# Reordering the first tiles of an attention and GLU kernel: split first load, square root first, copies on one engine, K by chunk

## The chip, the cores and the metric

The kernel runs on one core of a Trainium2 chip. The metric is the device time in microseconds (us) of an execution. Each execution also has a **span**, from its first to its last instruction, given to 0.1 us. Engines: PE (TensorE; PEld is its weight load, which overlaps), VectorE (DVE), ScalarE (ACT), GpSimd (POOL), SyncE (SP).

## The reference, cut to what matters

```python
xn = layernorm(x)                      # x: 1 x 2048 x 640, bf16
qkv = xn @ wqkv                        # wqkv: 640 x 1920
# 32 heads of 20; each position attends to 8 positions, 2 apart
o = softmax(q . k over the window) applied to v
out = x + o @ wo + ((xn @ w_gate) * (xn @ w_up)) @ w_down    # hidden width 1536
```

## The kernel before

The 2048 rows are 16 tiles of 128. Each tile gets a layernorm in place; tiles 0 to 3 are then transposed on PE through PSUM and copied to SBUF, the later ones by transposing transfers. Q and K of the first tiles are projected tile by tile while the rest of x is still normalised. The contraction of 640 goes in five chunks of 128, and the weights of Q and of K come in five loads each, one per chunk.

```python
x_load(1, "act"); x_load(0)                 # tile 1 on ScalarE's queue, tile 0 on SyncE's
for c in range(5): wqkv_load(0, c)          # Q's weight chunks, SyncE
x_load(2); x_load(3)
for c in range(5): wqkv_load(1, c)          # K's weight chunks, SyncE
...
def ln_aggr(t):                             # tiles other than 1: statistics on VectorE
    bn_aggr(mv, st)                         # DVE
    activation(sd, mv[:, 1:2], Sqrt)        # ACT
def ln_sums(t, k):                          # tile 1: sum (k=0), squares (1), square root (2) on ACT
    ...
def ln_copy(t, ...):                        # PSUM -> SBUF after the transposes
    parts = ((("act", 0, 1), ("dve", 1, 3), ("act", 3, 5)),    # tile 0
             (("dve", 0, 2), ("act", 2, 5)),                   # tile 1
             (("act", 0, 5),), (("act", 0, 5),))[t]
...
warm(10)                                    # 10 matmuls of 512 columns on zeros
ln_stats_a(0); ln_stats_b(0)
ln_sums(1, 0)
ln_aggr(0)
ln_sums(1, 1); ln_sums(1, 2)
ln_apply(0); ln_pe(0); ln_copy(0)           # normalise, transpose, copy
ln_apply(1)
warm(2, 128)
# then Q of tile 0 (tile 1 transposed after its chunk 2), Q of tile 1, K of tile 0
# (tile 2 transposed after chunk 2), K of tile 1 (tile 3 transposed after chunk 3)
```

Each instruction waits only for what its operands need.

## Time and profile before

| | before |
|---|---|
| time, median of the first 3 executions | 254.13 us (254.0 to 254.83) |
| span of the profiled one | 252.5 us |
| PE busy, share of the span | 249.1 us, 99% |
| first projection of tile 0 starts | 6.18 us |
| first projection of tile 2 starts | 12.68 us |
| PE's last work ends | 250.19 us |

PE works without a break from the first transpose on. So the end of PE is the start of its useful work plus a fixed 244 us, unless a gap opens. Two markers tell how the opening went: the first projection of tile 0, and the first projection of tile 2, by which the whole rearranged part is over. The order of SyncE's transfers (start, length of issue, what, count):

```profile
0.75 0.40 SPq L293 DMA_DIRECT2D XST<-in_A_x_dram  x1
1.20 2.33 SPq L293 DMA_DIRECT2D WQKV<-in_A_wqkv_dram  x5
3.57 0.91 SPq L293 DMA_DIRECT2D XST<-in_A_x_dram  x2
4.52 2.33 SPq L293 DMA_DIRECT2D WQKV<-in_A_wqkv_dram  x5
```

Q's five weight chunks are issued from 1.20 us on, one each 0.47 us; K's from 4.52.

### The profile page before, as it was taken

To read this page: it belongs to the slowest core of one execution; us is meant where nothing else is said; L and a number is where in the kernel's file an instruction comes from. 1 tells how busy PE (TensorE), PEld (TensorE's weight loads), DVE (VectorE), ACT (ScalarE), POOL (GpSimd) and SP (SyncE) were. 2 spreads that over 40 slices of the span, in tenths; PEclk is the share of its full clock that TensorE was granted. 3 is DMA by queue.
4 is the path that set the end of the run, shared out by engine and by line. 5 is a ranking of instruction groups with operands and counts; after the bars stand their busy time and mean duration, and the time that the engine had idled before them with its cause. 6 is when DMAs were issued, how large, how long until landed. Compare 5 with 4: busy or idle time off the path is not lost.

```text
span 252.5 us, 3929 instructions
## 1 busy us (share of the span) xinstructions
PE 249.1 (99%) x1623; PEld 149.3 (59%) x1623; DVE 214.7 (85%) x251; ACT 114.8 (45%) x204; POOL 35.9 (14%) x44
## 2 busy tenths in 40 slices
PE   8999999999999999999999999999999999999996
PEld 3999855555544444444444457764445777777775
DVE  4799999999999854999999974999999999993221
ACT  6577775555555557555555553135555112112000
POOL 1000001044515430003411110100000010111000
DMA  6969889956677471536379940393000021330511
GB/s 195 330 144 175 120 217 373 280 116 120 122 145 125 83 139 29 201 132 124 57 137 319 435 108 6 37 348 55 0 0 0 3 28 24 55 44 10 104 52 53
DMA packets 25649, 31.84 MB, mean 126 GB/s; under 512 B 9856, under 2 KB 22144, under 8 KB 25600
## 3 DMA queue, kind: packets, MB, share of 16 engines
q1 hardware_dynamic: 19104, 22.07, 28.4%
q0 software_dynamic: 6240, 9.31, 23.1%
q8 instruction: 12, 0.20, 0.3%
q10 hardware_dynamic: 288, 0.23, 0.3%
q14 instruction: 5, 0.04, 0.0%
HBM read 14.42 MB, written 4.59 MB: 75 GB/s over the span
## 4 chain that ended last, share of the span: by engine, by line
PE 99%; DVE 0%; issue 0%
PE PS L643 41%; PE PS L674 29%; PE PS L471 17%; PE PS L486 4%; PE PS L497 2%; PE PS L504 2%; PE PS L449 2%; PE PS L430 1%; DVE FOUT L688 0%; DVE ZERO L296 0%; DVE EPSC L297 0%
## 5 line engine op out<-in xcount | busy, mean ns | idle before, releaser
L643 PE MATMUL PS<-XNT,WG 128*128 128x512 bf16 x240 | 59.6, 379 | 0.0
L643 PE MATMUL PS<-XNT,WU 128*128 128x512 bf16 x240 | 59.6, 379 | 0.0
L610 DVE TENSOR_TENSOR PVB<-VO,ATB 128x10240 f16<-128x10240 bf16 x8 | 43.9, 5486 | 0.1
L471 PE MATMUL PS<-XNT,WQKV 128*128 128x512 bf16 x200 | 43.3, 379 | 0.0
L674 PE MATMUL PS<-WD,HT 128*128 128x320 bf16 (+2 forms) x300 | 43.2, 294 | 0.0
L643 PEld LDWEIGHTS PS<-XNT,WU 128*128 128x128 bf16 x240 | 23.5, 98 | 28.3
L643 PEld LDWEIGHTS PS<-XNT,WG 128*128 128x128 bf16 x240 | 23.5, 98 | 28.1
L645 ACT ACTIVATE USX<-PS 128x512 bf16<-128x512 f32 x48 | 28.7, 597 | 22.2 <-PE PS L643 21.2
L674 PEld LDWEIGHTS PS<-WD,HT 128*128 128x128 bf16 x300 | 28.7, 98 | 11.0
L471 PEld LDWEIGHTS PS<-XNT,WQKV 128*128 128x128 bf16 x200 | 23.5, 118 | 19.5
L605 DVE TENSOR_TENSOR PVB<-PVB 128x5120 f16<-128x5120 f16 (+1 forms) x16 | 34.5, 2154 | 0.3
L538 POOL DMA_DIRECT2D LOG<-PE x24 | 21.7, 931 | 59.6 <-DMA LOG<-PE 59.6
L645 ACT ACTIVATE HT<-PS 128x512 bf16<-128x512 f32 x36 | 21.5, 597 | 16.7 <-PE PS L643 16.7
L683 ACT ACTIVATE FACC<-PS 128x640 f16<-128x640 f32 x12 | 8.5, 704 | 45.4 <-PE PS L674 45.4
L674 PE MATMUL PS<-WO,VO 128*128 128x320 bf16 (+2 forms) x165 | 27.1, 295 | 0.0
L674 PEld LDWEIGHTS PS<-WO,VO 128*128 128x128 bf16 x165 | 15.9, 98 | 6.0
L527 DVE TENSOR_TENSOR PP<-QH,KH 128x2048 f16<-128x2048 bf16 x16 | 19.1, 1216 | 0.0
L527 DVE TENSOR_TENSOR TMP<-QH,KH 128x2048 f16<-128x2048 bf16 x16 | 19.0, 1216 | 0.0
L532 DVE TENSOR_TENSOR PP<-PP,TMP 128x4096 f16<-128x4096 f16 x8 | 18.3, 2288 | 0.2
L688 DVE TENSOR_TENSOR FOUT<-PS,XR 128x320 bf16<-128x320 f32 (+2 forms) x9 | 4.1, 454 | 16.6 <-PE PS L674 16.6
L698 POOL DMA_DIRECT2D out_dram<-FACC x6 | 7.1, 1186 | 76.5 <-ACT FACC L683 76.5
L538 POOL DMA_DIRECT2D PE<-PP x8 | 8.7, 1090 | 60.7 <-DVE PP L533 60.7
(67 smaller groups left out, 229.5 us busy)
## 6 DMA issues: line engine op xcount, KB each, us to landing
PE<-PP POOLq DMA_DIRECT2D x8, 512.0 KB, 5.0
ATB<-LOG SPq DMA_DIRECT2D x8, 512.0 KB, 4.8
LOG<-PE POOLq DMA_DIRECT2D x24, 128.0 KB, 2.7
WG<-in_B_w_gate_dram SPq DMA_DIRECT2D x5, 384.0 KB, 6.2
WU<-in_B_w_up_dram SPq DMA_DIRECT2D x5, 384.0 KB, 12.4
WD<-in_B_w_down_dram SPq DMA_DIRECT2D x1, 1920.0 KB, 10.0
out_dram<-in_A_x_dram SPq DMA_DIRECT2D x1, 1920.0 KB, 9.4
out_dram<-FACC POOLq DMA_DIRECT2D x6, 320.0 KB, 4.7
```

What stands on the lines that cost most here:

```text
L471: op("pe", (lambda l, x, c: lambda e: e.matmul(PS[:, b, :], l, x, start=(c == 0), stop=(c == NCH - 1)))(l, x, c), r=[l, x], w=[PS[:, b, :] ...
L486: op("pe", (lambda o, l, x, st, sp: lambda e: e.matmul(o, l, x, start=st, stop=sp))(o, l, x, st, sp), r=[l, x], w=[o], name=f"pp{which}_{m ...
L527: return (1.22, lambda: op("dve", lambda e: e.tensor_tensor(o, qw, kw, ALU.mult), r=[q, k], w=[o], name=f"prod{h}_{p}_{c}"))
L532: (2.3, lambda: op("dve", lambda e: e.tensor_tensor(a, a, b, ALU.add), r=[a, b], w=[a], name=f"psum{h}_{p}")),
L538: op("pool", lambda e: e.dma_start(o, i, accum_op=ALU.add), r=[o, i], w=[o], dma=True, name=name)
L605: return lambda: op("dve", lambda e: e.tensor_tensor(o, x, y, ALU.add), r=[x, y], w=[o], name=f"{name}_{b}")
L610: lambda: op("dve", lambda e: e.tensor_tensor(PVB[:], vw, aw, ALU.mult), r=[v, a], w=[PVB[:]], name=f"pv_{b}")),
L643: op("pe", (lambda l, x, c: lambda e: e.matmul(PS[:, b, :], l, x, start=(c == 0), stop=(c == NCH - 1)))(l, x, c), r=[l, x], w=[PS[:, b, :] ...
L645: op("act", lambda e: e.activation(o, PS[:, b, :], ACT.Copy), r=[PS[:, b, :]], w=[o], name=f"guev{which}_{m}_{j}")
L674: op("pe", (lambda l, x, i, b, wid: lambda e: e.matmul(PS[:, b, 0:wid], l, x, start=(i == 0), stop=(i == n - 1)))(l, x, i, b, wid), r=[l, ...
L683: op("act", (lambda o, i: lambda e: e.activation(o, i, ACT.Copy))(o, i), r=[PS[:, b - 1, :], PS[:, b, :]], w=[o], name=f"fin{t}")
L698: stores.append(op("pool", lambda e: e.dma_start(d, f, accum_op=ALU.add), r=[f, ("out",)], w=[("out", t)], dma=True, name=f"oacc{t}"))
```

## The change

The intent is to start the useful work of PE earlier. Tile 0 comes in two halves on two queues; its square root goes ahead of tile 1's sums on ScalarE; its copies all go to VectorE, so that none waits behind those sums; tile 1 is transposed later, in two pieces; K of tiles 0 and 1 is done chunk by chunk for both tiles together. The diff, cut to its core:

```diff
-    x_load(1, "act")
-    x_load(0)
+    for half, eng in ((0, "sp"), (1, "act")):
+        dst = XST[:, 0, half * DHALF:(half + 1) * DHALF]
+        dma(dst, xhbm[0:TS, half * DHALF:(half + 1) * DHALF], w=[dst], name=f"xh{half}", eng=eng)
+    x_load(1)
     for c in range(NCH):
         wqkv_load(0, c)
...  (w_gate and w_up: one transfer each instead of five; each half's statistics read their half only)
-        for c0, c1 in ((0, 128), (128, D)) if t == 0 else ((0, D),):
+        for c0, c1 in {0: ((0, 128), (128, D)), 1: ((0, 256), (256, D))}.get(t, ((0, D),)):
...
-        parts = ((("act", 0, 1), ("dve", 1, 3), ("act", 3, NCH)), ...
+        parts = ((("dve", 0, 1), ("dve", 1, 3), ("dve", 3, NCH)), ...
...
-    warm(10)
+    warm(9)
     ln_stats_a(0)
     ln_stats_b(0)
+    ln_aggr(0)
     ln_sums(1, 0)
-    ln_aggr(0)
...  (Q and K of tiles 0 and 1)
+    proj_tile(0, [(0, 0)], bm, {(4, 0): lambda: ln_pe(1, 0, 2), (4, 3): lambda: tr(1, 2)})
+    part_evac(0, 0, 1, 0, 4, 0, 0)
+    proj_tile(0, [(1, 2)], bm)
+    part_evac(0, 1, 1, 0, 4, 2, 0)
+    ln_apply(3)
+    proj_tile(1, [(0, 3), (1, 4)], bm, {(3, 0): lambda: tr(2), (4, 0): lambda: tr(3)})
```

More of the change, by code (lines that the diff above doesn't have):

```diff
@@ L343, in late_loads @@
         for T, src in ((WG, B_w_gate), (WU, B_w_up)):
-            for c in range(NCH):
-                dma(T[:, c], src[c * 128:(c + 1) * 128, :], w=[T[:, c]], name="ld_w")
+            dma(T[:], src.rearrange("(c p) n -> p c n", p=128), w=[T[:]], name="ld_w")
     def down_loads():
@@ L367, in ln_stats_a @@
         x, st = XST[:, t % NXS, :], STATS[:, t % 2, 0:12]
-        op("dve", lambda e: e.bn_stats(st[:, 0:6], x[:, 0:DHALF]), r=[x], w=[st], name=f"bna{t}")
+        op("dve", lambda e: e.bn_stats(st[:, 0:6], x[:, 0:DHALF]), r=[x[:, 0:DHALF]], w=[st], name=f"bna{t}")
     def ln_stats_b(t):
@@ L373, in ln_stats_b @@
         x, st = XST[:, t % NXS, :], STATS[:, t % 2, 0:12]
-        op("dve", lambda e: e.bn_stats(st[:, 6:12], x[:, DHALF:D]), r=[x], w=[("stb", t)], name=f"bnb{t}")
+        op("dve", lambda e: e.bn_stats(st[:, 6:12], x[:, DHALF:D]), r=[x[:, DHALF:D]], w=[("stb", t)], name=f"bnb{t}")
     def ln_aggr(t):
@@ L424, in ln_apply, with ln_pe @@
             late_loads()
-    def ln_pe(t):
-        for c in range(NCH):
+    def ln_pe(t, c0=0, c1=NCH):
+        for c in range(c0, c1):
             o = tp_view(t, c, c + 1)[:, 0, :]
@@ L432, in ln_copy @@
     def ln_copy(t, only=(0, 1, 2)):
-        parts = ((("act", 0, 1), ("dve", 1, 3), ("act", 3, NCH)), (("dve", 0, 2), ("act", 2, NCH)), (("act", 0, NCH),),
+        parts = ((("dve", 0, 1), ("dve", 1, 3), ("dve", 3, NCH)), (("dve", 0, 2), ("act", 2, NCH)), (("act", 0, NCH),),
                  (("act", 0, NCH),))[t]
@@ L487, in proj_part, with proj_tile @@
                r=[l, x], w=[o], name=f"pp{which}_{m}_{t}_{c}")
-    def proj_tile(which, t, b, bm, col, at=None):
-        for c in range(NCH):
-            if at is not None and at[0] == c:
-                at[1]()
+    def proj_tile(which, tiles, bm, at={}):
+        for c, (t, b) in [(c, tb) for c in range(NCH) for tb in tiles]:
+            col = (2 * which + t) * TS
             for m in range(NCH):
+                if (c, m) in at and t == tiles[0][0]:
+                    at[c, m]()
                 o = PS[:, b, m * TS:(m + 1) * TS] if m < 4 else PS[:, bm, col:col + TS]
                 l, x = wcols(which, c, m), XNT[:, c, t * TS:(t + 1) * TS]
-                st, sp = c == 0 and m in (0, 4), c == NCH - 1 and m in (3, 4)
+                st = c == 0 and (m == 0 or m == 4 and t == tiles[0][0])
+                sp = c == NCH - 1 and (m == 3 or m == 4 and t == tiles[-1][0])
                 op("pe", (lambda o, l, x, st, sp: lambda e: e.matmul(o, l, x, start=st, stop=sp))(o, l, x, st, sp),
@@ L724, in ln_next, with ln_start, tr @@
         ln_apply(t)
-    def tr(t):
-        ln_pe(t)
-        if t != 2:
-            ln_copy(t)
-        ln_stats_a(t + 1)
-        ln_stats_b(t + 1)
-        ln_aggr(t + 1)
-        if t == 2:
-            ln_copy(t)
-        if t < 3:
-            ln_apply(t + 1)
+    def ln_start(t):
+        ln_stats_a(t)
+        ln_stats_b(t)
+        ln_aggr(t)
+    def tr(t, c0=0):
+        ln_pe(t, c0)
+        ln_copy(t)
+        if t == 1:
+            ln_start(2)
+            ln_stats_a(3)
+            ln_stats_b(3)
+            ln_rstd(2)
+            ln_apply(2, lambda: ln_aggr(3))
     n_ln = [4]
-    t_ln = [12.6]
+    t_ln = [11.9]
     def ln_pace(t):
@@ L749, in ln_pace @@
             t_ln[0] += 1.45
-    tp = 6.8
-    for t0 in (0, 2, 4):
-        bm = bank() if t0 == 4 else None
-        if t0 == 2:
-            bank_ring[:] = [5, 0, 6, 7, 2, 1, 3, 4]
-            bm = bank()
-        order = ((0, 0), (0, 1), (1, 0), (1, 1)) if t0 < 4 else ((0, 0), (1, 0), (0, 1), (1, 1))
-        at = {(0, 0): (3, lambda: tr(1)), (1, 0): (3, lambda: tr(2)), (1, 1): (4, lambda: tr(3))}
-        for which, dt in order:
+    bm = 1
+    proj_tile(0, [(0, 0)], bm, {(4, 0): lambda: ln_pe(1, 0, 2), (4, 3): lambda: tr(1, 2)})
[4 more added lines that the diff above has]
+    proj_tile(1, [(0, 3), (1, 4)], bm, {(3, 0): lambda: tr(2), (4, 0): lambda: tr(3)})
+    ln_start(4)
+    for t in (0, 1):
+        part_evac(1, t, 1, 0, 4, 3 + t, 0)
+    ln_pace(12.0)
+    for u in (0, 1):
+        part_evac(u, 0, 2, 4, 1, bm, 2 * u * TS)
+    tp = 11.9
+    bank_ring[:] = [5, 0, 6, 7, 2, 1, 3, 4]
+    for t0 in (2, 4):
+        bm = bank()
+        for which, dt in ((0, 0), (1, 0), (0, 1), (1, 1)):
             t = t0 + dt
             b = bank()
-            if t0 == 0:
-                if bm is None:
-                    bm = bank()
-                proj_tile(which, t, b, bm, (2 * which + t) * TS, at.get((which, t)))
-            else:
-                proj_part(which, t, (0, 1), b, 0)
-                proj_part(which, t, (2, 3), b, 2 * TS)
-                proj_part(which, t, (4,), bm, (2 * which + dt) * TS)
+            proj_part(which, t, (0, 1), b, 0)
+            proj_part(which, t, (2, 3), b, 2 * TS)
+            proj_part(which, t, (4,), bm, (2 * which + dt) * TS)
             part_evac(which, t, 1, 0, 4, b, 0)
```

## The prediction

> **What bounds the kernel now.** I read the page's busy shares first, then the chain that ended last, then the first 13 us in order of time, then the tail. The page says that TensorE (PE) is the bound:
>
> ```profile
> PE 249.1 (99%) x1623; PEld 149.3 (59%) x1623; DVE 214.7 (85%) x251; ACT 114.8 (45%) x204; POOL 35.9 (14%) x44
> ```
>
> 99% hides that some of this PE work is filler. The chain in order of time (start, length, what) shows it:
>
> ```profile
> 1.00 4.45 PE PS L449 x10
> 5.45 0.21 PE PS L430
> 5.65 0.03 issue
> 5.68 0.54 PE PS L430 x4
> 6.23 0.11 PE PS L449 x2
> 6.34 0.88 PE PS L497 x15
> ...
> 250.19 0.02 issue
> ```
>
> L449 is the warm-up on a tile of zeros, L430 the transposes of the first x tiles, L497 the first projections. From the first transpose to 250.19 us the chain never leaves PE but for 0.03 us: PE works back to back for 245 us. So a later stage can give nothing, and VectorE's 85% is off the path. Only two things can move the end: when the real PE work starts, and a new gap. What sets the start is the chain of the first tile, here in the order of time:
>
> ```profile
> 3.06 0.49 DVE L368 BATCH_NORM_STATS2 STATS<-XST 128x6 f32<-128x320 bf16 x1 [1.75 <-DMA XST<-in_A_x_dram]
> 3.47 0.47 DVE L374 BATCH_NORM_STATS2 STATS<-XST 128x6 f32<-128x320 bf16 x1
> 3.74 0.74 ACT L388 ACTIVATE XNS<-XST 128x640 bf16<-128x640 bf16 x1 [1.50 <-DMA XST<-in_A_x_dram]
> 3.98 0.21 DVE L380 BATCH_NORM_AGGREGATE MV<-STATS 128x2 f32<-128x12 f32 x1
> 4.48 0.28 ACT L381 ACTIVATE SD<-MV,EPSC 128x1 f32<-128x1 f32 x1
> 4.79 0.17 DVE L400 RECIPROCAL SD<-SD 128x1 f32<-128x1 f32 x1 [0.61 <-ACT SD L381]
> 4.99 0.64 DVE L415 TENSOR_SCALAR XNS<-XST,MV,SD 128x128 bf16<-128x128 bf16 x2
> 5.36 0.10 PEld L430 LDWEIGHTS PS<-IDENT,XNS 128*128 128x128 bf16 x1 [0.82 <-DVE XNS L415]
> 5.60 0.29 ACT L393 ACTIVATE SD<-MV,EPSC 128x1 f32<-128x1 f32 x1
> 5.80 0.26 ACT L443 ACTIVATE XNT<-PS 128x128 bf16<-128x128 bf16 x1
> 6.12 0.94 PEld L497 LDWEIGHTS PS<-XNT,WQKV 128*128 128x128 bf16 x15
> ```
>
> Tile 0 lands at 3.06; its mean and variance are known at 4.19 (3.98 + 0.21); but its square root starts only at 4.48, since ScalarE is busy with tile 1's sum (3.74 + 0.74 = 4.48): about 0.25 us lost. After the transposes the copy of chunk 0 waits again for ScalarE, which is on tile 1's square root (5.60 to 5.89).
>
> **What the Trainium skill says.** (1) "TensorE: Matmul & The Clock Gate", Part 1: the array runs at half rate until a free-running window of about 3.4 us was busy, so the moment of the change varies from run to run. The trace agrees on the two rates: a warm-up matmul of 512 columns takes 0.43 us in the sequence, the first 15 projections of 128 columns 0.059 us each (0.88 / 15), and between them, at about 5.9 us, PE changes. (2) "DMA: Bandwidth & Descriptors", Issuing engines are not separate DMA queues: two queues share the 16 engines, and save only issue time. In the trace one SyncE issue takes 0.40 to 0.47 us, so that saving counts here. The same page, Specifications, wants 512 bytes or more per transfer; half an x row is 640, which is allowed. (3) "ScalarE: Activation LUTs", What ACT_TABLE_LOAD costs: 280 ns + 0.833 ns per element with a pointer bias, 186 + 0.833 without. The trace has 812 ns for the 640-wide square (formula 813), 736 for the 640-wide sum (719) and 288 for the square root of one column (281): it agrees, so I use the trace's durations.
>
> **The change, part by part.**
> 1. *Tile 0 in halves on two queues; tile 1 second on SyncE.* In the old order tiles 0 and 1 shared the engines from the start: by 3.0 us some 0.33 MB had moved, both tiles together, and tile 0 was usable at 3.06. Now 160 KB of tile 0 are ahead of tile 1. From the GB/s of 0.2 us stretches about 65 KB had moved by 2.2 and 192 KB by 2.6; with 0.2 us to landing, the first half is usable at about 2.55 and the second, issued at 1.01 and sharing with tile 1, at about 2.95. The second statistics (3.47 before) start then: **0.5 us** earlier.
> 2. *Square root of tile 0 ahead of tile 1's sums.* It follows the aggregate by 0.25 instead of 0.50: **0.25 us**. The chain is then: statistics b 2.95, aggregate 3.46, square root 3.71, reciprocal 4.02, normalise 4.22 with its first piece done at 4.53 and its second at 4.86.
> 3. *Nine warm-up matmuls for ten.* Nine end at about 1.00 + 9 x 0.428 = 4.85, so the first transpose starts at 5.36 - 0.43 = 4.93, not at 4.59 that the data would allow. Of the 0.75 us won in 1 and 2, the first transpose gets only **0.43**. The other four have their data (4.86) and follow at the cold 0.107 us each: 5.03 to 5.46; the two small warm-ups last to 5.67.
> 4. *Copies of tile 0 on VectorE.* Transposed data can be copied some 0.31 us after its transpose starts (314 ns, the longest in the trace); chunk 0 at 5.25, about 0.22 us for 128 columns (my estimate from 0.29 for 256), done by 5.5. The other two end near 5.8 and 6.05. So projection starts when PE is through with the small warm-ups: 5.67 instead of 6.18, **0.5 us** earlier, a little of it perhaps at the cold rate.
> 5. *Tile 1 transposed after 20 projections instead of 15, in two pieces.* ScalarE now begins tile 1's sums after the square root, near 3.9 (3.74 before): sum 3.9, square 4.74, square root 5.68 to 5.97. VectorE is free of copies at 6.05; reciprocal 6.07, first 256 columns normalised by 6.6. PE has done 20 projections at 5.67 + 20 x 0.056 = 6.8 or 6.9. No wait. From the second transpose (6.9) to the copied chunk the old trace takes 0.25 + 0.29 + 0.05; PE has five projections and three transposes to cover it, 0.45 us: tile 1's Q starts near 7.5, after a gap of some 0.1. Before it started at 7.33 + 10 x 0.056 = 7.89. The lead is **about 0.4 us**.
> 6. *K of tiles 0 and 1 by chunk.* The same 50 matmuls, transposes of tiles 2 and 3 later among them. Tile 2's normalised data: statistics of 2 and 3 follow on VectorE from 7.4, apply ends near 10.0; PE asks at 7.5 + 1.4 + 30 x 0.056 = 10.6. Its copy on ScalarE stands behind both Q evictions and ends near 11.8; PE asks at 12.26. Both hold, with about 0.5 us to spare. The weights of K: their bytes stand in the same order, the engines moved about 320 GB/s, so the first chunk lands near 7.3 and is asked for at 8.9.
> 7. *Up and gate weights in one transfer each.* Same bytes, some 4 us less issue time on SyncE (5.3 us for ten, about 1 for two). They are used from 72.6 us on, long after landing: **nothing**.
>
> Sum: start 0.5 us earlier, 0.1 given back before tile 1's Q, nothing after: 0.4 to 0.45 us. Hence 254.13 - 0.43 = **253.7 us**.
>
> **Rivals.** (a) *The wait moves to tile 1.* Its sums start later than before while PE comes to it earlier; the margin in step 5 is about 0.2 us. If tile 1's load or ScalarE is late by 0.3 or more, part of the gain is lost: 253.9 to 254.1. For it: three ScalarE instructions in a row with no slack. Against: its transposes were put off by five projections. (b) *The clock.* If PE turns warm at the same absolute time or later, projections begun 0.5 us earlier run at half rate at first and the gain is 0.2 to 0.3: 253.85. If it turns early, the warm-up ends early too, the data bound of 4.59 counts, and the gain is up to 0.55: 253.55. The old runs spread from 254.0 to 254.83, which is more than the whole expected gain. (c) *ScalarE's queue in order.* Q evictions now stand behind tile 3's square root (near 9.7), and tile 2's copy behind them; if tile 3's statistics slip by over 0.5 us PE waits before its second pair of tiles: 254.1 or more. (d) *A hidden transfer or a later engine.* Later tiles go by transposing transfers; the last attention piece on VectorE ends at 229.71, and PE reaches the tiles that need it over 10 us later. A lead of 0.4 us meets nothing there.
>
> **Range and chances.** The gain is bounded by the time between the first landing and the first projection, about 3 us in all, so 2% (5.1 us) faster is impossible, and 2% slower would take a stall ten times the parts moved. 253.7, range 253.2 to 254.3: 0.55 us of gain plus noise below, a lost gain plus noise above.
>
> **What would show it.** Right: first statistics near 2.6 and second near 3.0; square root within 0.3 of the aggregate; first transpose near 4.9, directly after the ninth warm-up; first projection near 5.7; no PE gap over 0.15 us after it; the end of PE near 249.8 (250.19 before). Wrong: the second half landing at 3.3 or later (step 1), a PE wait for XNS of tile 1 (step 5) or for ScalarE's copies of tile 2 (step 6), cold projections past 6.5 us (rival b), or a gap anywhere after 13 us, which I think there is none of.

## The result, and the profile after

The changed kernel took 254.26 us (median of 6, 253.94 to 254.5), the kernel before 254.2 us (median of 6). The ratio of the mean time of the fast runs of one to that of the other's in the same rounds, which is not quite the ratio of the medians, is 0.9998, with a 95% interval of 0.9984 to 1.0012: the same. The value lies just inside the range foretold, but the gain of 0.43 us did not come.

```profile
PE 248.1 (98%) x1607; PEld 149.2 (59%) x1622; DVE 215.1 (85%) x254; ACT 113.9 (45%) x202; POOL 35.9 (14%) x44
```

PE's count fell by more than the one warm-up taken out: this trace lacks some matmul records (the chain shows stretches of 49 with 0.05 us between them where there are 50). So the loss of busy time is not to be read as work saved. The weight loads of the opening, in order of time, show the loss better:

```profile
5.62 0.95 PEld L500 LDWEIGHTS PS<-XNT,WQKV 128*128 128x128 bf16 x15
6.91 0.32 PEld L500 LDWEIGHTS PS<-XNT,WQKV 128*128 128x128 bf16 x5 [0.34 <-DVE XNS L416]
7.17 0.15 PEld L431 LDWEIGHTS PS<-IDENT,XNS 128*128 128x128 bf16 x2
```

The first projection's weight load is at 5.62 (6.12 before; its matmul at 5.68 for 6.18): the forecast start. Fifteen projections follow (chunks 0, 1, 2), then a hole of 0.34 us, then the five of chunk 3, then tile 1's transposes at 7.17 where I had them near 6.85. In the kernel before, the transposes follow the fifteen projections and all else follows them, without a hole:

```profile
7.01 0.31 PEld L430 LDWEIGHTS PS<-IDENT,XNS 128*128 128x128 bf16 x5
7.28 2.85 PEld L497 LDWEIGHTS PS<-XNT,WQKV 128*128 128x128 bf16 x50
```

And at the end of the opening and of the kernel (changed kernel; chain; start, length, what):

```profile
6.94 0.45 PE PS L500 x5
7.39 0.11 PE PS L431 x2
7.50 0.17 PE PS L500 x3
7.67 0.17 PE PS L431 x3
7.84 3.32 PE PS L500 x57
...
12.83 11.17 PE PS L487 x200
...
250.17 0.02 issue
```

Against the chain before, 12.83 stands for 12.85, and 250.17 for 250.19. The lead of 0.50 us at the first projection is 0.02 us at tile 2 and stays so.

**What the hole waits for.** The profile puts it down to tile 1's normalised data (XNS, L416). That can't be: in program order these five matmuls stand ahead of tile 1's transposes and use tile 0's data and weight chunk 3. It named the instruction that ended last before the start (0.36 us from 6.51, so 6.87). The transfer that the five do need is the fourth of Q's loads. SyncE's list of the changed kernel and the issue-to-landing view of that one load (last column, us) give its landing:

```profile
1.67 2.32 SPq L293 DMA_DIRECT2D WQKV<-in_A_wqkv_dram  x5
4.03 0.91 SPq L293 DMA_DIRECT2D XST<-in_A_x_dram  x2
4.98 2.33 SPq L293 DMA_DIRECT2D WQKV<-in_A_wqkv_dram  x5
```

```profile
WQKV<-in_A_wqkv_dram SPq DMA_DIRECT2D x1, 160.0 KB, 3.7
```

Issued at 3.07 (1.67 + 3 x 0.47), landed 3.7 us later: 6.8 us. The packed trace also holds the instruction in which PE waits for this load's semaphore: it ends at 6.89, 0.02 us before the weight load at 6.91. In the kernel before chunk 3 landed at 6.6 and PE came to it at 7.33. In the changed kernel it lands at 6.8 and PE comes to it at 5.68 + 15 x 0.06 = 6.6: 0.5 us sooner by the early start, and some 0.2 us more because tile 1's five transposes no longer stand ahead of it.

Tile 1, now second on SyncE, has also pushed the issue of all ten weight loads back by 0.46 us. The landing of chunk 3 did not follow: it was at 6.21 to 6.83 in the ten traces with this order (all of the table below but e_actq, e_best and the two of the kernel before), and at 6.63 and 6.87 in the kernel before. That of K's fourth chunk did: 10.23 to 11.40, against 10.07 and 10.13. So at chunk 3 it is PE's earlier asking that makes the hole.

The Trainium skill, "DMA: Bandwidth & Descriptors", Why a DMA increments its semaphore by 16 and not by 1, says that the engines of one transfer finish independently and that it has landed only when all have. The trace agrees: of the 16 parts of this chunk eight had landed by 5.56 us, fifteen by 6.30, the last at 6.81.

Two things come close together here: chunk 3 at 6.8 and tile 1's data at 6.87. PE needs the second only five projections after the first, so without the hole it would have come to it near 6.85 and hardly waited; in another execution either can come last. So the experiments had to take them away one by one, and both.

### The profile page after: what moved, and what is told of

Read it like the earlier page. It is cut to its first block, busy times and chain, and to the rows that moved or that the text cites. A ratio compares the mean times of both kernels' runs of the same rounds, so it can differ in the third digit from the quotient of the medians.

```text
span 252.4 us, 3908 instructions
## 1 busy us (share of the span) xinstructions
PE 248.1 (98%) x1607; PEld 149.2 (59%) x1622; DVE 215.1 (85%) x254; ACT 113.9 (45%) x202; POOL 35.9 (14%) x44
## 4 chain that ended last, share of the span: by engine, by line
PE 96%; ACT 1%; DMA 1%; DVE 1%; issue 0%
PE PS L646 41%; PE PS L677 29%; PE PS L472 17%; PE PS L487 4%; PE PS L507 2%; PE PS L500 2%; DMA XST<-in_A_x_dram 1%; ACT XNS L391 0%; PE PS L431 0%; ACT XNS L389 0%; DVE STATS L369 0%; DVE STATS L375 0%; DVE XNS L416 0%; ACT SD L394 0%; ACT SD L382 0%
## 5 line engine op out<-in xcount | busy, mean ns | idle before, releaser
L646 PE MATMUL PS<-XNT,WG 128*128 128x512 bf16 x229 | 57.3, 379 | 0.6
L472 PE MATMUL PS<-XNT,WQKV 128*128 128x512 bf16 x196 | 43.0, 379 | 0.2
L472 PEld LDWEIGHTS PS<-XNT,WQKV 128*128 128x128 bf16 x200 | 23.5, 118 | 19.5
## 6 DMA issues: line engine op xcount, KB each, us to landing
WU<-in_B_w_up_dram SPq DMA_DIRECT2D x1, 1920.0 KB, 17.3
```

Of the source, the lines that this page charges most:

```text
L472: op("pe", (lambda l, x, c: lambda e: e.matmul(PS[:, b, :], l, x, start=(c == 0), stop=(c == NCH - 1)))(l, x, c), r=[l, x], w=[PS[:, b, :] ...
L646: op("pe", (lambda l, x, c: lambda e: e.matmul(PS[:, b, :], l, x, start=(c == 0), stop=(c == NCH - 1)))(l, x, c), r=[l, x], w=[PS[:, b, :] ...
```

## The experiments

Theory A: the lead is lost at the front, to the landing of Q's weights and then to tile 1's data. Rival B: to tile 1's data alone, as the profile names it. Rival C: the front keeps its lead and a later stage gives it back.

The table gives, from each trace, the start of the first projection of tile 0 (P0), of tile 1's transposes (T1), of the first projection of tile 2 (P2), and the end of PE, in us; then the mean span of all executions, and that of the kernel before in the same rounds on the same chip (number of executions in brackets). T1 comes after 15 projections in the kernel before and in b_dma, after 20 in the others. Each trace is one execution, and the two of the changed kernel differ by 0.56 us at P2; so the waits inside a trace count for more here than a few tenths between two traces.

| run | P0 | T1 | P2 | PE end | span | before beside it |
|---|---|---|---|---|---|---|
| kernel before, first trace | 6.18 | 7.06 | 12.68 | 250.19 | 252.5 (1) | |
| b2: before again | 6.14 | 7.01 | 12.60 | 250.10 | 252.4 (1) | |
| changed kernel | 5.68 | 7.23 | 12.67 | 250.17 | 252.43 (6) | |
| a2: changed again | 5.85 | 7.40 | 13.23 | 250.74 | 252.68 (5) | 252.54 (9) |
| e_q34 | 5.56 | 6.92 | 12.49 | 250.00 | 252.90 (4) | 252.60 (7) |
| e_t1 | 5.68 | 7.08 | 12.52 | 250.17 | 252.43 (4) | 252.60 (7) |
| e_warm10 | 5.98 | 7.41 | 12.87 | 250.45 | 252.62 (4) | 252.60 (7) |
| e_actq | 5.54 | 7.26 | 12.71 | 250.21 | 252.55 (4) | 252.60 (7) |
| e_oldsqrt | 5.84 | 7.17 | 12.74 | 250.25 | 252.62 (4) | 252.54 (9) |
| e_actcopy | 6.40 | 7.55 | 12.99 | 250.69 | 252.90 (4) | 252.54 (9) |
| e_free | 5.53 | 6.71 | 12.24 | 249.75 | 252.58 (6) | 252.55 (11) |
| b_dma | 6.16 | 7.03 | 13.64 | 251.15 | 253.18 (6) | 252.55 (11) |
| e_ktile | 5.55 | 7.04 | 13.43 | 251.12 | 253.47 (4) | 252.55 (11) |
| e_best | 5.89 | 7.39 | 12.85 | 250.35 | 252.72 (6) | 252.54 (12) |

Over all rounds the changed kernel's 11 spans have a mean of 252.55 and the 28 of the kernel before on three chips one of 252.56. A single execution of the kernel before spans 252.2 to 253.2.

**e_q34: no wait for chunks 3 and 4 of Q in tile 0** (wrong result).

```diff
-                l, x = wcols(which, c, m), ...
+                l, x = wcols(which, 2 if which == 0 and t == 0 and c > 2 else c, m), ...
```

> The changed kernel, but Q of tile 0 uses the weights of chunk 2 in place of chunks 3 and 4, so PE does not wait for those two loads there (wrong result on purpose). Theory A (the lead of 0.5 us is lost to the landing of Q's weight chunk 3 at about 6.8 us, which the profile puts down to tile 1's normalised data): the 5 matmuls that started at 6.94 start near 6.6, the first transpose of tile 1 near 6.9 instead of 7.23, tile 1's Q near 7.57 instead of 7.90, and the first projection of tile 2 near 12.35 to 12.45 instead of 12.67; span 252.1 to 252.2 where the changed kernel has 252.4. Rival B (the stall is tile 1's normalised data, as the attribution says): the matmuls at 6.94 stay there, first projection of tile 2 at 12.67, span 252.4.

In its trace the twenty projections run through with no group of five set apart:

```profile
5.50 1.26 PEld L500 LDWEIGHTS PS<-XNT,WQKV 128*128 128x128 bf16 x20
6.91 0.11 PEld L431 LDWEIGHTS PS<-IDENT,XNS 128*128 128x128 bf16 x2 [0.15 <-DVE XNS L416]
```

P0 is at 5.56, T1 at 6.92 and P2 at 12.49. T1 and the direction are as theory A had them; of the expected 0.22 to 0.32 us at P2, 0.18 came (the rest of the 0.31 us won at T1 went to K's first chunk, which landed at 9.07 just after PE came to it). Rival B's T1 of 7.23 did not. PE's 0.15 us before T1 are now rightly tile 1's data. But this trace decides less than it seems to: in this execution chunk 3 itself landed at 6.21, before PE would have come to it (5.56 + 15 x 0.06 = 6.46), so no hole was due there with the right weights either. The spans (252.3, 252.9, 254.1, 252.3) are too scattered to say anything.

**e_t1: no wait for tile 1's statistics** (wrong result).

```diff
-            i = XNS[:, t % NXN, c * 128:(c + 1) * 128]
+            i = XNS[:, 0 if t == 1 else t % NXN, c * 128:(c + 1) * 128]
```

> The changed kernel, but the transposes of tile 1 read tile 0's normalised data, so PE does not wait for tile 1's statistics (wrong result on purpose). Theory A (weight chunk 3): nothing moves, matmuls of chunk 3 at 6.9, first projection of tile 2 at 12.67, span 252.4. Rival B (tile 1's normalised data): the stall of 0.3 us is gone, first projection of tile 2 near 12.35, span 252.1.

Chunk 3 kept its hole, which rival B excludes, since no matmul here needs tile 1's statistics:

```profile
5.62 0.98 PEld L500 LDWEIGHTS PS<-XNT,WQKV 128*128 128x128 bf16 x15
6.76 0.32 PEld L500 LDWEIGHTS PS<-XNT,WQKV 128*128 128x128 bf16 x5 [0.16 <-DVE SD L401]
```

The chunk landed at 6.65 this time, and PE's own wait for it ends at 6.74; the profile names tile 1's reciprocal (SD, L401), once more the instruction that happened to end last. Theory A's "nothing moves" was too strong: the chunk landed 0.16 us sooner than in the first trace and P2 came 0.15 us sooner. That lead then met something later that I had ruled out. The weight loads near 29 us:

```profile
28.93 0.12 PEld L507 LDWEIGHTS PS<-XNT,WQKV 128*128 128x128 bf16 x1
29.25 0.37 PEld L472 LDWEIGHTS PS<-XNT,WQKV 128*128 128x128 bf16 x3 [0.21 <-DMA XNT<-XNS]
```

L472 is the first wide projection of tiles 8 to 11; its weight load waited 0.21 us for the transposing transfer of tile 11, PE itself lost 0.14 (43.31 us for these 200 matmuls instead of 43.17), and it ended at 250.17 as in the changed kernel. So rival C also holds in some executions.

**e_warm10: ten warm-up matmuls again.**

```diff
-    warm(9)
+    warm(10)
```

> The changed kernel with ten warm-up matmuls again: the first transpose starts near 5.35 and the first projection near 6.1, as in the kernel before. Theory A: chunk 3 still starts at 6.9, the stall before it shrinks from 0.3 to near 0, first projection of tile 2 at 12.67, span 252.4: the early start was worth nothing. Rival C (the early start is worth its 0.4 us and something else, late in the kernel, gave it back): span 252.8, first projection of tile 2 near 13.1.

Inconclusive. P0 was 0.3 us later and P2 0.2 us later, between the two theories. The twenty projections took 1.55 us of weight loads instead of about 1.2, with no hole: by the two rates given under a2, PE's slow clock held on until they were about half done, and that covered the landing of chunk 3.

**e_actq: chunks 3 and 4 of Q on ScalarE's queue.**

```diff
-        wqkv_load(0, c)
+        wqkv_load(0, c, "act" if c > 2 else "sp")
```

> The changed kernel with Q's weight chunks 3 and 4 issued on ScalarE's queue right after the second half of tile 0, so that they are issued near 1.4 and 1.8 us instead of 3.1 and 3.5. Theory A, if the landing is set by the place in the queue: chunk 3 lands before 6.5, PE's stall before it is gone, tile 1's transposes near 6.9, first projection of tile 2 near 12.35 to 12.45, span 252.1 to 252.2. Theory A, if the landing is set by the rate of the 16 engines: the other chunks or tile 1 land later by as much, and the stall moves to them; span 252.4 or more. Rival B: tile 1's load is delayed by the shared engines, span 252.5 or more.

The second case of theory A, and rival B's mechanism with it. Chunk 3 landed at 4.75 and chunk 4 at 5.6, but tile 1 at 4.5 instead of 3.4 and chunk 1 at 6.0 instead of 4.9. PE stopped 0.31 us before chunk 1, and tile 1's transposes came at 7.26. The Trainium skill, "DMA: Bandwidth & Descriptors", Issuing engines are not separate DMA queues, says that transfers of all queues interleave on the same engines; the trace fits that: the hole moved from one chunk to another.

**a2 and b2: both kernels again**, unchanged.

> The changed kernel once more, with the most rounds, to see whether the stall in front of weight chunk 3 belongs to the kernel or to one execution. So far its chunk 3 landed at 6.8 us and the same chunk at 6.2 and 6.65 in two near copies of it. Theory A (the front is held by whichever of two things comes last, Q's weight chunk 3 or tile 1's normalised data, which is ready at 6.86): first projection near 5.6, PE idle 0.1 to 0.4 us in all before tile 1's transposes, first projection of tile 2 at 12.45 to 12.7; span mean 0.1 to 0.2 under that of the kernel before on this chip. Rival C (no loss at the front, a later stage gives the lead back): tile 2 near 12.3, end of PE near 250.2 all the same.

> The kernel before once more, for a second trace: first projection at 6.1 to 6.2, no PE idle after it, first projection of tile 2 at 12.6 to 12.8 (12.68 in the first trace), span 252.2 to 252.7. If it varies by 0.3 us or more with no change at all, the whole forecast gain is of the size of this variation.

In its two traces the kernel before repeats within 0.1 us. But the spans of its 28 executions differ by up to 1.0 us, so the expectation's last sentence holds: the whole forecast gain is of the size of this variation. The changed kernel doesn't repeat even in its traces: P2 is at 13.23, 0.56 us later than in its first (this execution was the slowest of the five: 253.0, the others 252.5 to 252.7). The cause is the wait for chunk 4, this time named by the profile:

```profile
5.75 1.66 PEld L500 LDWEIGHTS PS<-XNT,WQKV 128*128 128x128 bf16 x20
7.34 0.15 PEld L431 LDWEIGHTS PS<-IDENT,XNS 128*128 128x128 bf16 x2
7.90 0.21 PEld L500 LDWEIGHTS PS<-XNT,WQKV 128*128 128x128 bf16 x3 [0.40 <-DMA WQKV<-in_A_wqkv_dram]
```

Chunk 4 was issued near 3.55 and landed 4.3 us later, at 7.85. In the kernel before it landed at 7.1 and 7.3 and was asked for at 7.6. The clock is to be seen too: twenty projections took 1.66 us, where twenty at the fast rate take 1.12. An estimate from these: at 0.107 us slow and 0.056 fast, some ten of them ran slow. Here it did not set the time, since PE then still waited 0.40 us for chunk 4; in e_warm10, where PE waited for none of these loads, it did. The span mean is 0.14 above the kernel before's where 0.1 to 0.2 below was expected.

**e_free: both waits of the front taken away, and K's too** (wrong result; edit of e_t1 as well).

```diff
-                l, x = wcols(which, c, m), ...
+                l, x = wcols(0, min(c, 2), m), ...
```

> The changed kernel with both suspected waits of the front taken away at once (wrong result on purpose): all projections of tiles 0 and 1 use the weights of Q's chunks 0 to 2, and the transposes of tile 1 read tile 0's data. Theory A: 20 projections run through from 5.6 to 6.75, tile 1's transposes follow at once, tile 1's Q waits only for its copy on VectorE and starts near 7.5, first projection of tile 2 at 12.25 to 12.35: the forecast lead of 0.4 us, and a span 0.25 to 0.4 under the kernel before's on the same chip, unless the transposing transfer of tile 11 (landed between 28.3 and 29.5 in the traces so far) stops PE near 29 us. Rival C (the lead is lost later whatever the front does): tile 2 near 12.3 but the span mean within 0.1 of the kernel before's.

The forecast opening appears, though chunk 3 landed at 6.83 here too: T1 at 6.71, P2 at 12.24, a lead of 0.44 us, and it holds to the end of PE. Its weight loads, then its chain:

```profile
5.47 1.25 PEld L500 LDWEIGHTS PS<-XNT,WQKV 128*128 128x128 bf16 x20
6.66 0.15 PEld L431 LDWEIGHTS PS<-IDENT,XNS 128*128 128x128 bf16 x2
```

```profile
12.40 11.17 PE PS L487 x200
...
249.75 0.02 issue
```

So the front's waits are what took the lead in the changed kernel's traces, and nothing late takes it in this one. The spans are another matter: 252.0, 253.2, 251.8, 252.6, 252.1, 253.8. Three lie below every span of the kernel before, but the mean is 252.58, so theory A's 0.25 to 0.4 us did not come, and by the mean alone rival C's mark (within 0.1) was met. With 2.0 us between the fastest and the slowest of six, the mean decides neither. What the other three executions lost I can't say, since only one execution of a run has a trace.

**e_oldsqrt: tile 1's sum ahead of tile 0's square root again.**

```diff
-    ln_aggr(0)
     ln_sums(1, 0)
+    ln_aggr(0)
     ln_sums(1, 1)
```

> The changed kernel with tile 1's sum issued ahead of tile 0's square root again, as before. Theory A: with tile 1 landing at 3.44 its sum ends about when tile 0's aggregate does, so the square root starts near 4.1 instead of 3.98 and costs the first projection 0.1 us at most, while tile 1's normalised data is ready near 6.7 instead of 6.86; what PE then waits for is weight chunk 3, so the span stays within 0.1 us of the changed kernel's, 252.3 to 252.5. Rival D (the new order of the square root is what brings the early start): first projection at 5.9 or later, span 252.6 or more.

The square root started at 4.29 (4.1 expected, 3.98 in the changed kernel) and P0 at 5.84, 0.16 later; the span mean is 252.62 for a2's 252.68 on the same chip. Theory A's own numbers missed (P0 at most 0.1 later, 252.3 to 252.5), and rival D's span of 252.6 was reached. But beside a2 no loss is seen, and PE's last wait at the front was for chunk 4, which landed at 7.36. So giving this part back cost nothing that these runs can show, and what the order of the square root is worth stays open.

**e_actcopy: first and last copies of tile 0 on ScalarE again.**

```diff
-    parts = ((("dve", 0, 1), ("dve", 1, 3), ("dve", 3, NCH)), ...
+    parts = ((("act", 0, 1), ("dve", 1, 3), ("act", 3, NCH)), ...
```

> The changed kernel with the first and last copies of tile 0 on ScalarE again. ScalarE is in tile 1's sums until its square root ends at 6.27, so the first copy starts near 6.2 and the first projection near 6.5 instead of 5.6. The 15 projections before chunk 3 then end at 7.4, after its landing and after tile 1's data: no stall there, tile 1's transposes near 7.7 instead of 7.23. Theory A: first projection of tile 2 near 13.1 instead of 12.67, span 252.8 to 252.9. If the early start were not what the copies buy, the span would stay at 252.4.

As expected to 0.15 us: P0 at 6.40, waiting 0.78 us for ScalarE's copy, no hole at chunk 3, P2 at 12.99, mean span 252.90, 0.22 over a2. With tile 1's sums behind the square root, ScalarE can't make these copies in time, so their move is needed by the rest of the change.

**b_dma: the new load order alone, in the kernel before.** The edit is the first hunk of the change, with each half's statistics reading its half.

> The kernel before with one part of the change alone: tile 0 in halves on two queues, tile 1 second on SyncE, each half's statistics waiting for its half only. The square root of tile 0 starts near 4.3 (4.48 before), first projection near 5.95 (6.18), tile 1's transposes near 6.85, chunk 3 near 7.1, behind its landing at 6.6 to 6.9, chunk 4 near 7.4, at about its landing of 7.1 to 7.4. Theory A: the lead of 0.2 us survives in executions where the weights land early, first projection of tile 2 at 12.45 to 12.7, span 0 to 0.2 under the kernel before's. Rival E (the loads alone make the loss, since tile 0's halves and tile 1 now delay the weights): span above the kernel before's.

This shows what the load order costs in the kernel before, where K goes tile by tile. Tile 1 landed at 3.77 this time, so ScalarE's sum held the square root to 4.52 as before, and P0 was at 6.16: no gain. Q's chunks 3 and 4 landed at 6.55 and 7.02, before PE came to them. Then K of tile 0, still tile by tile, ran into K's weights, which SyncE now issues 0.46 us later:

```profile
10.96 0.47 PE L499 MATMUL PS<-XNT,WQKV 128*128 128x128 bf16 x5 [0.41 <-DMA WQKV<-in_A_wqkv_dram]
11.66 1.59 PE L499 MATMUL PS<-XNT,WQKV 128*128 128x128 bf16 x25 [0.23 <-DMA WQKV<-in_A_wqkv_dram]
```

In the kernel before, K's last chunk landed at 10.65 just after PE came to it, so there was no margin to give. The mean span is 0.63 us over the kernel before's, and the ratio 1.0022 (1.0006 to 1.0039). Rival E is right for this kernel. In the two traces of the changed kernel PE waits for none of K's weights.

**e_ktile: the changed kernel with K of tile 0 before K of tile 1.**

```diff
-    proj_tile(1, [(0, 3), (1, 4)], bm, {(3, 0): lambda: tr(2), (4, 0): lambda: tr(3)})
+    proj_tile(1, [(0, 3)], bm)
+    proj_tile(1, [(1, 4)], bm, {(3, 0): lambda: tr(2), (4, 0): lambda: tr(3)})
```

> The changed kernel with K of tile 0 finished before K of tile 1, as before, instead of by chunk. K's chunks landed at 8.5, 9.5, 10.0, 10.35 and 10.8 in the changed kernel's trace; tile 0 alone asks for them every 0.28 us from 9.3 on, so PE waits some 0.1 to 0.4 us in all before chunks 2 to 4, tile 2's first projection is at 12.8 to 13.1 and the span 0.1 to 0.4 over the changed kernel's. If K by chunk buys nothing, tile 2 stays at 12.67.

More than expected: P2 at 13.43, mean span 253.47, 0.92 us over the kernel before's and, over the changed kernel's mean of 252.55 from other chips, about as much. PE's weight loads waited at each of K's five chunks, 0.12 to 0.33 us. A further 0.17 us was a wait for tile 2's copy, which is not K's weights: with this edit tile 2's transposes start only 1.2 us ahead of P2 (1.7 in the changed kernel). K by chunk asks for a new chunk every 0.56 us instead of 0.28; that is what keeps the late weights off the path.

**e_best: tile 1 and Q's chunk 4 behind the second half of tile 0 on ScalarE's queue**, an attempt to beat both kernels.

```diff
-    x_load(1)
+    x_load(1, "act")
     for c in range(NCH):
-        wqkv_load(0, c)
+        wqkv_load(0, c, "act" if c == NCH - 1 else "sp")
```

> The changed kernel with tile 1 behind the second half of tile 0 on ScalarE's queue, and Q's weight chunk 4 behind it there; SyncE then issues chunk 0 at 1.2 instead of 1.67, chunk 3 at 2.6 instead of 3.1, and every load after Q two issues (0.9 us) earlier. Theory A (the lead is lost because the change puts tile 1 ahead of the weights on SyncE, so that each chunk is issued 0.45 us later than before while PE asks for it 0.5 us earlier): tile 1 lands near 3.8, before ScalarE is free at 4.2; chunks 3 and 4 land by 6.5, K's chunks by 9.5; PE waits only for tile 1's data near 6.9 and for its copy, so the first projection of tile 2 is at 12.35 to 12.5 against 12.67 to 13.2 in the two traces of the changed kernel; the span mean is 0.1 to 0.3 under the changed kernel's (252.4 and 252.7 in its two sets) and near or just under that of the kernel before on this chip. If issue order does not set the landing, chunk 3 or another chunk lands near 6.8 again and tile 2 is at 12.67 or later.

A miss. The weights came as meant. Chunk 4, issued 1.7 us sooner on the other queue, landed at 5.7 (7.02 to 7.85 in the ten traces with the order of the change), so the issue does move a landing; but chunk 3, issued 0.5 us sooner, landed at 6.45, inside its range in those traces (6.21 to 6.83). But tile 1, expected near 3.8, landed at 4.6, and its chain became the wait. ScalarE's sum and PE's transposes:

```profile
4.65 0.74 ACT L389 ACTIVATE XNS<-XST 128x640 bf16<-128x640 bf16 x1 [0.30 <-DMA XST<-in_A_x_dram]
7.39 0.11 PEld L431 LDWEIGHTS PS<-IDENT,XNS 128*128 128x128 bf16 x2 [0.18 <-DVE XNS L416]
```

T1 is at 7.39 and the mean span 252.72 for 252.54 beside it. No version with a right result beats the kernel before clear of noise.

## Why the prediction was right or wrong

The range held, by luck, as noise around no gain and not around 0.43 us.

1. *The start (steps 1 to 4)* was right where it counts. The first projection came at 5.68 for 5.67 forecast. Within it, the first half landed at 2.79 for 2.55, so the first statistics started at 2.82 and the second at 3.23 for 2.95; the square root at 3.98 for 3.71, though it followed the aggregate by 0.24 as foretold. Nine warm-ups hid that: the first transpose was at 4.88, as soon as they were through, and tile 0's data had come only just in time for it (its weight load at 4.87 waited for that data). So the match of 0.01 us is partly luck.
2. *Step 5 failed*: "PE has done 20 projections at 5.67 + 20 x 0.056 = 6.8 or 6.9. No wait." The sum lacks a term, the landing of Q's own weights. I computed the landing of K's weights and forgot Q's. Moving tile 1's transposes behind chunk 3 brought that chunk's turn forward by 0.73 us (7.33 to 6.6), start included. Chunk 3 landed at 6.8 and chunk 4 at 7.26 in the first trace, 7.85 in the second; T1 came at 7.23 and 7.40. The step's other term was late too: tile 1's data came at 6.87 for 6.6, since its square root was at 5.98 for 5.68. Step 1 does not count that its load order moves the weights' issue back by 0.46 us; for Q's chunk 3 no later landing is seen, for K's chunks it is. The sign of being wrong that was named, "a PE wait for XNS of tile 1", was printed by the profile of the changed kernel, but there it was not the wait. With the waits removed, e_free shows the forecast lead (12.24 for 12.26). The gap of "some 0.1" before tile 1's Q was there: it started at 7.90 after the copy on VectorE, 0.11 after PE was free. So in the first trace 0.37 lost to the hole and 0.11 to the copy make up the 0.5 us of lead.
3. *Step 6* held in the sense that no wait came, but its size was off: K's first chunk landed at 8.5, not 7.3. The margin was thin enough that without K by chunk PE stops (b_dma, e_ktile).
4. *Step 7*: the two big transfers landed 9.3 and 17.3 us after their issue near 34 us, long before their use near 72. I did not test that part alone.
5. *Rival (b)*, the clock, is real: it counted in e_warm10 and was hidden behind chunk 4 in a2. *Rival (a)* named the right place and the wrong wait in the first trace, and the right one in e_q34 and e_best. *Rival (d)* was wrong in saying that a lead of 0.4 us meets nothing later: in e_t1 the weight load at 29.25 waited 0.21 us for tile 11's transposing transfer, and in e_actcopy the one at 29.78 waited 0.26 us for the same.

What stays open: whether the executions without a trace lost their lead to the same waits; why only half of e_free's executions show its lead in the span, and how much of the scatter of single executions (252.2 to 253.2 us for the kernel before) is clock and how much is landing of transfers.

## What to carry to other kernels

An engine that starts earlier asks for everything earlier: before moving its start, list the landing time of each operand that it will ask for, and its margin, not just the ones that were waited for. Moving a load ahead on a queue delays the issue of all behind it (here by 0.46 us); whether the landings follow is to be looked up for each (here K's did and Q's chunk 3 did not). Where a profile names a releaser, check in program order that the waiting instruction needs it. And before an experiment's trace is read as proof, check that the wait which it takes away was due in that execution at all.

## What the Trainium skill lacked or had wrong

- "DMA: Bandwidth & Descriptors", Why a DMA increments its semaphore by 16 and not by 1: it says that the engines finish independently, but gives no size for the spread. Here the last of 16 parts of a 160 KB load came 1.25 us after the eighth (5.56 and 6.81), and which load was hit changed from run to run: chunk 4 of Q landed between 7.1 and 7.85 us in the two traces of each kernel.
- "TensorE: Matmul & The Clock Gate", Back-to-back issue gap: it gives 81 ns per matmul of 128 columns and 131 ns for 512 in a stream of weight load and matmul pairs. The trace of the kernel before has 56 ns (2.79 us for 50) and 216 ns (43.17 us for 200) in such a stream, which are the figures that the section gives for a matmul by itself.
- The same page, Part 4: it says that the fast clock does not engage for transposes. Here five transposes between projections took 0.28 us, 56 ns each, the rate of the projections around them. Whether transposes by themselves would bring the fast clock about was not tested.
- The same page, Part 1: the clock's release at a varying moment is as it says. In e_t1 nine warm-up matmuls took 3.49 us and in a2 4.02; in a2 the projections were still partly slow after 5.75 us. The profile's granted clock read 1.0 in all of these, so it does not show this.
